# Attention, eight experts and a mixing layer in one kernel: two experts' rows turned by VectorE, and steps re-ordered on three engines

## The chip, the cores and the metric

The program runs on one core of a Trainium2 chip. That core has five engines that run side by side and in order, each through its own queue of instructions: TensorE (PE in the profile; its weight loads are shown apart as PEld), VectorE (DVE), ScalarE (ACT), GpSimd (POOL) and SyncE (SP), which here only starts transfers. Sixteen DMA engines move data between the chip's large memory and the on-chip memory. The metric is the device time of one execution in microseconds; the time of a kernel is the median over its runs.

## The reference

Three stages follow one another: attention, a layer of eight experts in which each token goes to one of them, and a layer that mixes tokens.

```python
# attention: B=2, H=8, S=768, D=64
keep  = is_global | is_local                       # 8 global keys, 96 local ones
a     = softmax(where(keep, q @ k.T * scale - slope * dist, -1e9))
x     = (a @ v) as (B, S, 512)
# experts: E=8, hidden size 1024
logits = x @ w_gate;  local_gate = sigmoid(x @ w_local)
e[s]   = argmax(logits[s]) if s == 0 or local_gate[s] < 0.5 else e[s-1]
x[s]   = softmax(logits[s])[e] * (relu(x[s] @ w1[e]) @ w2[e])
# mixing
theta = x @ w_theta
y     = w_tok_r @ (x cos theta) + w_tok_i @ (x sin theta)
u     = x + y
out   = u + relu(u @ w_ch)
```

The tables of the last stage (w_theta, w_tok, w_ch) arrive as 64-bit floats; the kernel turns them into pairs of 32-bit ones.

## The kernel before

**Attention (0 to about 97 us).** Twelve blocks of 128 tokens. Beside it runs the routing, by pairs of blocks: a chain of small steps that goes back and forth between TensorE and VectorE, two letters each in the list TAIL: `ch` choice, `ro` rows, `sc` scan, `oh` one-hot, `ho`, `po` positions, `pl` place, `mk` marks, `sl` slots, `tk` tokens; `rk` ranks the experts by their number of tokens, `en` writes the lists of tokens (`xidx`) from which rows are gathered.

**The leader (about 96 to 113 us).** When half of the tokens are routed, 128 rows of the expert that then leads are computed ahead. Its hidden layer is cut into eight groups f of 128 units: `ha` and `hb` are the two halves of a first product (L783), `hr` the relu on ScalarE (L788), `ya` and `yb` the two halves of the second product (L794). TAIL writes out by hand in which order these and the last routing steps are issued, and so the order on every engine. Each TensorE product in it waits in TensorE's queue for what it needs, and everything behind it waits too. When `en` has written the lists, GpSimd gathers the first expert's rows (`xg`, L1046), TensorE turns them (`tr`, L1341) and the first expert starts.

**Experts, in order of their number of tokens (115 to 288 us).** Expert r gets at most RCAP[r] = 288, 256, 240, 208, 192, 176, 160, 144 tokens, in tiles of up to 128 rows. Its hidden layer is cut into eight half groups; u = 8r + f counts them from 0 to 63. For each u:

- `mm1` (L1524 for r < 4, L1505 above): the product with w1 into `h`. For r < 4 weights and rows are split into a high and a low part: `w1s` from the loaded `raw` (high part by ScalarE, L1369, low part by VectorE, L1370), and three products.
- `relu`: `hh` by ScalarE (L1553, L1559) and the low part `hl` by VectorE (L1555, L1562); rows beyond the full tile go as `hx` (L1554, L1561).
- `mm2` (L1580): the product with w2, split as `w2s` (`h2`, L1486, by ScalarE; `l2`, L1487, by VectorE), into `o`. For each tile of rows three products follow one another: hh·h2, hh·l2, hl·h2. `mm2_few` (L1596) is the product of the few rows `hx` with `raw`.

For r < 4 the loop goes through u one by one, above it by pairs. TensorE gets the products of u+2 (or u+2 and u+3) ahead of `mm2` of u.

**Rows of the next expert.** `x_tr` at f = 2 and 3 (r < 4) or f = 2 (r of 4 and more) turns a gathered tile of 128 rows x 512 features into features x rows: four products with the identity per tile (L1341) into PSUM and a copy (L1344, L1347, L1349). It then lets GpSimd gather the tile three further on (L1046); three tiles `xg` are held.

**Conversion steps.** `job` is a generator that turns one piece of a 64-bit table into `jw` and then into the split tables (`wth`, `wtokr`, `wch`): per piece two ScalarE steps (L418, L428) and five VectorE steps (L419 to L431). `tick()`, called six times per u (twelve per pair), runs JRATE[r]/4.5 (r of 1 to 3, not at f = 2, 3) or JRATE[r]/6 of a step, so JRATE sets how many of them fall into which expert. A ScalarE step of a job (L428) waits in ScalarE's queue for the VectorE step before it.

**Mixing (290 to 465 us).** For each of twelve blocks the expert results are gathered back from memory (L1774, L1783; for most blocks in four quarters of each row, which VectorE turns in 32 x 32 squares, L1798), and the products of theta (L1843), of the token mixing (L1929) and of w_ch (L1966) follow.

Other names: `yo` is an expert's result on its way to memory (L1631, L1633; stored by GpSimd, L1635), `y` the leader's (L1639), `ps` its tokens' probabilities (L1423), `jraw` the loaded piece of a table.

## Time and profile before

| | before |
|---|---|
| median of 3 runs | 467.28 us (467.28 to 467.78) |
| the profiled execution | 466.93 us, of it span 465.0 us |
| TensorE busy | 457.9 us (98%) |
| VectorE, ScalarE, GpSimd busy | 344.0 (74%), 262.3 (56%), 142.9 us (31%) |

The span runs from the first to the last instruction of the profiled execution. The page's first part gives each engine's busy time, the second cuts the span into 40 slices, the fourth follows the chain that ended last. Times in the rows below are microseconds from the start of the span; "x6" is a number of instructions taken together, and what stands in brackets at a row's end is the idle time before it and what ended that.

### The profile page before, as it was taken

The numbers are of one execution on the slowest core, as the hardware profiler recorded it, in microseconds if no ns is written. First come the engines' busy times: TensorE is split into PE (matmuls) and PEld (weight loads), VectorE is DVE, ScalarE is ACT, GpSimd is POOL, SyncE is SP. The second block draws the span as 40 slices with busy tenths as digits, with TensorE's granted clock in tenths as the row PEclk, the third lists the DMA queues.
The fourth block names the chain that finished last, engine by engine and source line by source line (L and its number), as shares of the span: only waits on it lengthen the run. The fifth ranks groups of instructions, "written<-read, shape, count | busy, mean of one in ns | idle before, by whom it ended". The sixth has DMA issues, their size and how long they took to land.

```text
span 465.0 us, 9578 instructions
## 1 busy us (share of the span) xinstructions
PE 457.9 (98%) x3346; PEld 378.7 (81%) x3346; DVE 344.0 (74%) x946; ACT 262.3 (56%) x623; POOL 142.9 (31%) x203
## 2 busy tenths in 40 slices
PE   8999999999999999999999999999999999999996
PEld 4677777788888898888787788888888888888886
DVE  5888889768687697887888776687997897741522
ACT  5988786822456666655755544556765665630300
POOL 8602313204032404040514302654874441000400
PEclk9999999999999999999999999999999999999999
DMA  8978577715957788788999993521253110000022
GB/s 241 367 231 248 184 240 253 252 47 158 356 167 225 265 296 270 257 277 270 318 348 307 305 312 132 165 91 48 79 152 109 43 49 24 0 35 34 28 87 93
DMA packets 61770, 85.60 MB, mean 184 GB/s; under 512 B 6248, under 2 KB 40296, under 8 KB 61720
## 3 DMA queue, kind: packets, MB, share of 16 engines
q1 hardware_dynamic: 52212, 62.06, 40.8%
q0 software_dynamic: 5552, 12.55, 8.8%
q10 hardware_dynamic: 3956, 10.36, 6.6%
q8 instruction: 27, 0.44, 0.4%
q14 instruction: 23, 0.19, 0.1%
HBM read 73.56 MB, written 11.38 MB: 183 GB/s over the span
## 4 chain that ended last, share of the span: by engine, by line
PE 90%; ACT 4%; DVE 3%; issue 1%; DMA 1%; POOL 0%; DVEq 0%
PE a L1929 22%; PE o L1580 15%; PE h L1524 10%; PE h L1505 8%; PE b L1966 7%; PE th L1843 7%; PE s L574 4%; PE x L653 3%; PE o L1596 3%; PE pt L629 3%; ACT pr L606 2%; PE tr L1341 1%; PE y L670 1%; DVE sm L596 1%; ACT ps L638 1%; PE h L783 1%
## 5 line engine op out<-in xcount | busy, mean ns | idle before, releaser
L1929 PE MATMUL a<-wtokr,z 128*128 128x512 f32 x480 | 85.3, 336 | 0.0
L1929 PEld LDWEIGHTS a<-wtokr,z 128*128 128x128 f32 x480 | 74.2, 188 | 10.0
L1580 PE MATMUL o<-w2s,hh 128*128 128x512 f32 x192 | 62.7, 406 | 0.0
L606 ACT ACTIVATE pr<-sm,st 128x256 f32<-128x256 f32 (+1 forms) x96 | 46.0, 483 | 15.3 <-DVE st L596 15.2
L1524 PE MATMUL h<-xT,w1s 128*128 128x288 f32 (+3 forms) x384 | 51.4, 284 | 0.5 <-DVE xT L1347 0.5
L1524 PEld LDWEIGHTS h<-xT,w1s 128*128 128x128 f32 x384 | 48.7, 189 | 3.4 <-issue 0.6
L1783 POOL DMA_INDIRECT xq<-yd,Lall x40 | 42.4, 1059 | 25.2 <-issue 9.8
L1487 DVE TENSOR_TENSOR w2s<-raw,w2s 128x512 fp32r<-128x512 f32 x56 | 38.5, 689 | 8.4 <-ACT w2s L1486 8.4
L596 DVE CUSTOM_DVE_ANT_0 sm<-s,bias 128x256 f32<-128x256 f32 (+1 forms) x96 | 34.0, 395 | 9.2 <-PE s L574 5.1
L1505 PEld LDWEIGHTS h<-xT,raw 128*128 128x128 f32 x256 | 37.0, 190 | 4.4 <-issue 3.9
L1505 PE MATMUL h<-xT,raw 128*128 128x192 f32 (+3 forms) x256 | 40.5, 311 | 0.0
L1580 PE MATMUL o<-w2s,hl 128*128 128x512 f32 x96 | 38.0, 396 | 0.0
L1580 PEld LDWEIGHTS o<-w2s,hh 128*128 128x128 f32 x192 | 32.4, 184 | 5.8 <-DVE w2s L1487 1.0
L1486 ACT ACTIVATE w2s<-raw 128x512 fp32r<-128x512 f32 x56 | 34.8, 626 | 2.9 <-DMA raw<-in_w_dram 1.4
L1635 POOL DMA_DIRECT2D yd<-yo x13 | 8.2, 634 | 79.1 <-ACT yo L1631 72.4
L1974 DVE SCALAR_TENSOR_TENSOR ob<-b,xTf 128x512 f32<-128x512 f32 (+1 forms) x16 | 8.8, 558 | 29.0 <-PE b L1966 25.7
L1370 DVE TENSOR_TENSOR w1s<-raw,w1s 128x512 fp32r<-128x512 f32 x32 | 22.0, 689 | 6.9 <-ACT w1s L1369 6.4
L574 PE MATMUL s<-kall,q 64*128 64x256 f32 (+1 forms) x192 | 26.1, 391 | 0.0
L629 PE MATMUL pt<-ident,pr 128*128 128x128 f32 x176 | 24.6, 278 | 0.2
L653 PE MATMUL x<-ps,vv 128*64 128x128 f32 x352 | 24.5, 279 | 0.0
L428 ACT ACTIVATE wtokr<-jw 128x512 fp32r<-128x512 f32 x15 | 9.5, 633 | 24.6 <-DVE jw L425 24.6
L1843 PE MATMUL th<-wth,xh 128*128 128x512 f32 x88 | 22.4, 396 | 0.0
(294 smaller groups left out, 944.3 us busy)
## 6 DMA issues: line engine op xcount, KB each, us to landing
raw<-in_w_dram SPq DMA_DIRECT2D x60, 512.0 KB, 5.4
vv<-in_pack_dram SPq DMA_DIRECT2D x10, 512.0 KB, 6.5
jraw<-in_w_tokT_dram ACTq DMA_DIRECT2D x10, 512.0 KB, 5.0
w<-in_w_dram SPq DMA_DIRECT2D x16, 256.0 KB, 5.4
kall<-in_pack_dram SPq DMA_DIRECT2D x10, 320.0 KB, 5.3
xd<-xt SPq DMA_DIRECT2D x12, 256.0 KB, 2.3
q<-in_pack_dram SPq DMA_DIRECT2D x11, 256.0 KB, 4.4
jraw<-in_w_tokT_dram ACTq DMA_DIRECT2D x10, 256.0 KB, 4.7
```

The lines of the kernel that those rows point to most:

```text
L574: PE.matmul(sp[hh][:, 0:W], lhsT=qs[n][half, j], rhs=kall[half, b, j, t * 160 + 160 - W : t * 160 + 160], start=True, stop=True,)
L596: V.tensor_tensor_reduce(out=sm[:, hh, 0:W], in0=ust[u]["s"][hh], in1=bias[:, 2 * j + hh], scale=-0.125, scalar=BIG, op0=ALU.add, op1=ALU.min,
L606: A.activation(pr[:, hh, 0:W], sm[:, hh, 0:W], AF.Exp, bias=st[:, hh : hh + 1], scale=-1.0, accum_out=sums[n][:, 2 * j + hh : 2 * j + hh + 1],
L629: PE.transpose(pt[:, hh, c], pr[:, hh, c * 128 : (c + 1) * 128], ident)
L653: PE.matmul(xp[64 * hh : 64 * hh + 64, j], lhsT=vv[:, i, h * 64 : (h + 1) * 64], rhs=ps[:, hh, c], start=(c == 0), stop=(c == nch - 1),)
L1487: V.tensor_tensor(l2, bb[:, o], f32(h2), op=ALU.subtract)
L1505: PE.matmul(hp[:, :N], lhsT=pieces[u // 2][1][:, j, o * 128 : (o + 1) * 128], rhs=x[:, j, :N], start=(j == 0), stop=(j == 3),)
L1524: PE.matmul(hp[:, :N], lhsT=wa[:, j], rhs=xa[:, j, :N], start=(k == 0), stop=(k == 11))
L1580: PE.matmul(out[:M], lhsT=ha[:, lo : lo + M], rhs=wa, start=(f == 0 and q == 0), stop=(f == 7 and q == 2),)
L1783: G.indirect_dma_start(xq[:, i * 128 : (i + 1) * 128], None, yd.rearrange("n (q w) -> (n q) w", q=4), bass.IndirectOffsetOnAxis(ap=yq[:, i ...
L1843: PE.matmul(th, lhsT=xa[:, j], rhs=wa[:, j], start=(n == 0), stop=(n == 11))
L1929: PE.matmul(acc[b][d][o], lhsT=za[:, d * 128 : (d + 1) * 128], rhs=wa[:, lo:hi], start=(t == 0 and n == 0 and (o == 0 or d % 2 == 0)), sto ...
```

## The change

Five edits stand together.

1. The rows of the last two experts (r of VX = 6 and more) are no longer turned by TensorE. A tile of 128 rows is gathered in four transfers of 128 quarter rows each (a tile of 32 or 16 rows in one), so that the quarters q of 32 rows lie on partitions 32q to 32q+31; one VectorE transpose of 32 x 32 squares per tile writes the rows into `xT`, and there is no copy out of PSUM. Features then lie in another order on the partitions, and w1 of these experts is loaded with rows in the same order. The indices of the quarters are worked out by `quarters`, four VectorE instructions at each u of 2 to 5.
2. JRATE: 1.2 and 1.3 become 1.5 and 1.6 for experts 1 and 2, and 2.7 and 2.3 become 2.3 and 2.1 for experts 4 and 5. The sum of steps stays.
3. In TAIL the leader's half products are cut apart and placed between the routing's products.
4. `mm2` puts hh·h2 of all tiles first and the low products behind them, and takes the two half groups of a pair together.
5. For u of 29 to 31 `split_w2` stands ahead of the ticks; in pairs the six ticks are spread 2, 2, 2 instead of 3, 3, 0.

```diff
-ri11 mk4 ha0 hb0 hr0 jt yt11 lg11 lc11 jt ha1 hb1 hr1 lt11 ld11 ya0 yb0 sl4 ch5 tk4 ha2 hb2 hr2 ro5 sc5 ys11 ya1 yb1 oh5
-ho5 ha3 hb3 hr3 po5 pl5 ya2 yb2 mk5 rk ha4 hb4 hr4 sl5 tk5 ya3 yb3 ha5 hb5 hr5 en ya4 yb4 ha6 hb6 hr6 ya5 yb5 ha7 hb7
+ri11 mk4 ha0 hb0 hr0 jt yt11 lg11 lc11 jt ha1 lt11 ld11 hb1 hr1 ya0 sl4 ch5 tk4 yb0 ro5 sc5 ys11 ha2 hb2 hr2 oh5 ho5
+ya1 yb1 po5 pl5 ha3 hb3 hr3 ya2 mk5 rk sl5 tk5 yb2 ha4 hb4 hr4 ya3 yb3 ha5 hb5 hr5 en ya4 yb4 ha6 hb6 hr6 ya5 yb5 ha7 hb7
...
-JRATE = (2.0, 1.2, 1.3, 3.0, 2.7, 2.3, 0.8)
+JRATE = (2.0, 1.5, 1.6, 3.0, 2.3, 2.1, 0.8)
...
+            order = "o (a p) f -> p (o a) f" if r < VX else "o (p a) f -> p (o a) f"
+            SP.dma_start(p[1], w1[bass.ds(ev, 1), :, c * 256 : (c + 1) * 256].rearrange(order, p=128))
...
+        if r < VX:
+            G.indirect_dma_start(xg[:M], None, xd[:], bass.IndirectOffsetOnAxis(ap=xidx[:M, r, i : i + 1], axis=0))
+            return
+
+        for k in range(-(-M // 32)):
+            idx = xq[:, k, r - VX, i : i + 1] if k < 2 else xq2[:, k - 2, r - VX : r - VX + 1]
+            G.indirect_dma_start(
+                xg[:, k * 128 : (k + 1) * 128],
+                None,
+                xd.rearrange("n (q w) -> (n q) w", q=4),
+                bass.IndirectOffsetOnAxis(ap=idx, axis=0),
+            )
...
+    def quarters(q):
+
+        o = slice(32 * q, 32 * q + 32)
+        for k in range(4):
+            p = slice(32 * k, 32 * k + 32)
+            dst, src = (xq[o, k, 0 : E - VX], xidx[p, VX:E, 0:2]) if k < 2 else (xq2[o, k - 2, 0 : E - VX], xidx[p, VX:E, 0])
+            V.tensor_scalar(dst, src, 4.0, float(q), op0=ALU.mult, op1=ALU.add)
...
+        if r >= VX:
+            k = -(-M // 32)
+            V.transpose(
+                f32(xh[:, :, i * 128 : i * 128 + 32 * k]).rearrange("p j (k a) -> p k j a", a=32),
+                xg[:, 0 : 128 * k].rearrange("p (k c j) -> p k j c", c=32, j=4),
+            )
+            gather_x(n + 3)
+            return
...
-            for i in range(RTILES[r]):
-                lo = i * 128
-                M = min(128, RCAP[r] - lo)
-                if width(r, i) == 128:
-                    out = yps[r][i]
-                    for q, (ha, wa) in enumerate(((hh, h2), (hh, l2), (hl, h2))):
...
+                        prods[0].append((out, hh[:, c], h2, u % 8 == 0, False))
+                        low = [(out, hh[:, c], l2, False, False), (out, hl[:, c], h2, False, u % 8 == 7)]
+                        for k in range(2):
+                            prods[1 if len(us) > 1 else 1 + k].append(low[k])
+            for out, ha, wa, first_, last_ in prods[0] + prods[1] + prods[2]:
+                PE.matmul(out, lhsT=ha, rhs=wa, start=first_, stop=last_)
...
+                    ahead = u + 3 >= 8 * FEW0
+                    if ahead:
+                        split_w2(u + 1)
...
-                mm2(u)
-                mm2(u + 1)
+                mm2(u, u + 1)
...
+            if u in range(2, 6):
+                quarters(u - 2)
```

On TensorE, in the third half group pair of expert 5 (`h` the first product, `tr` the turning of expert 6's two tiles, `o` the second product), before:

```order
L1505 MATMUL h<-xT_3652,raw_3717 128x176 x8
L1341 MATMUL tr<-ident,xg 128x128 x4
L1341 MATMUL tr<-ident,xg 128x32 x4
L1580 MATMUL o<-w2s_3841,hh 128x512
L1580 MATMUL o<-w2s_3842,hh 128x512
L1580 MATMUL o<-w2s_3841,hl 128x512
L1580 MATMUL o<-w2s_3854,hh 128x512
L1580 MATMUL o<-w2s_3855,hh 128x512
L1580 MATMUL o<-w2s_3854,hl 128x512
L1596 MATMUL o<-raw_3729,hx 64x256 x4
```

and now:

```order
L1537 MATMUL h<-xT_3680,raw_3748 128x176 x8
L1618 MATMUL o<-w2s_3865,hh 128x512
L1618 MATMUL o<-w2s_3879,hh 128x512
L1618 MATMUL o<-w2s_3866,hh 128x512
L1618 MATMUL o<-w2s_3865,hl 128x512
L1618 MATMUL o<-w2s_3880,hh 128x512
L1618 MATMUL o<-w2s_3879,hl 128x512
L1628 MATMUL o<-raw_3760,hx 64x256 x4
```

The eight `tr` products are gone (the same at expert 6 for expert 7's tiles), and the two products with a high part on both sides stand first.

On TensorE, in the leader's stretch between the slots of routing step 4 and the positions of step 5 (`small` are routing's products, `h` and `y` the leader's), before:

```order
L783 MATMUL h_1951<-lead_r,w_1416 128x128 x4
L283 LDWEIGHTS rcb
L283 MATMUL small<-identb,rcb 2x128
L284 LDWEIGHTS rcb
L284 MATMUL small<-identb,rcb 2x128
L794 MATMUL y_1931<-w_1416,lead_r 128x256 x2
L302 MATMUL small<-own_80,erow 128x16
L783 MATMUL h_1975<-lead_r,w_1416 128x128 x4
L318 LDWEIGHTS ones
```

and now:

```order
L800 MATMUL y_1931<-w_1416,lead_r 128x256
L286 LDWEIGHTS rcb
L286 MATMUL small<-identb,rcb 2x128
L287 LDWEIGHTS rcb
L287 MATMUL small<-identb,rcb 2x128
L789 MATMUL h_1960<-lead_r,w_1416 128x128 x4
L305 MATMUL small<-own_80,erow 128x16
L800 MATMUL y_1931<-w_1416,lead_r 128x256 x2
L321 LDWEIGHTS ones
```

Each routing product has come forward past half a group or a whole group of the leader's products, which now stand behind it.

On GpSimd, from the gather of expert 5's second tile to the store of the leader's rows, before:

```order
L1046 DMA xg<-xd,xall 48x512
L1046 DMA xg<-xd,xall 128x512
L1635 DMA yd<-yo 128x512
L1635 DMA yd<-yo 80x512
L1417 DMA ps<-pd,toks 128x1
L1423 DMA ps<-pd,toks 128x1
L1046 DMA xg<-xd,xall 32x512
L1046 DMA xg<-xd,xall 128x512
L1423 DMA ps<-pd,sidx 128x1
L1639 DMA yd<-y_107 128x512
```

and now:

```order
L1053 DMA xg<-xd,xall 48x512
L1058 DMA xg<-xd,toks 128x128 x4
L1667 DMA yd<-yo 128x512
L1667 DMA yd<-yo 80x512
L1449 DMA ps<-pd,toks 128x1
L1455 DMA ps<-pd,toks 128x1
L1058 DMA xg<-xd,toks 128x128 x5
L1455 DMA ps<-pd,sidx 128x1
L1671 DMA yd<-y_107 128x512
```

Two gathers of 128 rows have become four each; a store of results, probabilities and the leader's store are queued behind them as before.

## Rows read from the trace of the kernel before

**Rows 1.** The page, part 1: busy time, share of the span, instructions.
```profile
PE 457.9 (98%) x3346; PEld 378.7 (81%) x3346; DVE 344.0 (74%) x946; ACT 262.3 (56%) x623; POOL 142.9 (31%) x203
```
**Rows 2.** The page, part 4: the chain that ended last, by engine.
```profile
PE 90%; ACT 4%; DVE 3%; issue 1%; DMA 1%; POOL 0%; DVEq 0%
```
**Rows 3.** Windows, experts 1, 2, 5, 6: length; busy PE, PEld, DVE, ACT, POOL; clock; DMA share, GB/s.
```profile
140.50:164.60 24.10, 24.10 (x172) 21.42 (x169) 17.98 (x34) 16.36 (x35) 7.71 (x9) 1.00 0.76 248
164.60:187.30 22.70, 22.70 (x154) 20.23 (x153) 19.21 (x37) 14.95 (x32) 5.74 (x6) 1.00 0.84 280
...
232.50:253.40 20.90, 20.90 (x130) 16.43 (x128) 17.13 (x36) 12.86 (x27) 6.65 (x12) 1.00 0.98 330
253.40:272.20 18.80, 18.80 (x155) 15.32 (x153) 14.93 (x38) 9.94 (x20) 4.60 (x7) 1.00 0.91 299
```
**Rows 4.** Timeline of PE, experts 5 and 6: starts of half group pairs.
```profile
237.47 2.65 PE L1505 MATMUL h<-xT,raw 128*128 128x176 f32 x16
...
242.46 2.65 PE L1505 MATMUL h<-xT,raw 128*128 128x176 f32 x16
...
248.44 2.65 PE L1505 MATMUL h<-xT,raw 128*128 128x176 f32 x16
...
262.54 2.44 PE L1505 MATMUL h<-xT,raw 128*128 128x160 f32 x16
...
267.85 2.44 PE L1505 MATMUL h<-xT,raw 128*128 128x160 f32 x16
...
272.18 2.23 PE L1505 MATMUL h<-xT,raw 128*128 128x144 f32 x16
```
**Rows 5.** Groups by line: GpSimd's quarter gathers, a transpose, a small VectorE step.
```profile
L1783 POOL DMA_INDIRECT xq<-yd,Lall x40 | 42.4, 1059 | 25.2 <-issue 9.8 <-DVE xTf L1798 8.5 <-DMA yd<-y 5.7
...
L1798 DVE STREAM_TRANSPOSE xTf<-xq 128x512 f32<-128x512 f32 x10 | 7.1, 706 | 0.3 <-DMA xq<-yd,Lall 0.3
...
L1406 DVE TENSOR_SCALAR Lall<-yidx 32x10 int32<-32x10 int32 x16 | 2.6, 163 | 0.2
```
**Rows 6.** Timeline of DVE, where experts 6's and 7's rows are turned.
```profile
246.93 0.69 DVE L1487 TENSOR_TENSOR w2s<-raw,w2s 128x512 fp32r<-128x512 f32 x1 [0.74 <-ACT w2s L1486]
...
266.72 0.69 DVE L1487 TENSOR_TENSOR w2s<-raw,w2s 128x512 fp32r<-128x512 f32 x1 [2.59 <-ACT w2s L1486]
```
**Rows 7.** Timeline of POOL, experts 4 and 5.
```profile
224.80 1.13 POOL L1635 DMA_DIRECT2D yd<-yo  x2 [17.38 <-ACT yo L1631]
...
230.44 1.11 POOL L1046 DMA_INDIRECT xg<-xd,xall  x1 [0.30 <-PE o L1580]
...
235.13 0.59 POOL L1639 DMA_DIRECT2D yd<-y  x1 [2.33 <-DVE jw L419]
235.71 0.15 POOL L1550 MEMSET hx<- 128x32 f32 x1
```
**Rows 8.** Timeline of PE, first half groups of expert 0.
```profile
119.06 0.79 PE L1580 MATMUL o<-w2s,hh 128*128 128x512 f32 x2
...
120.62 0.89 PE L1580 MATMUL o<-w2s,hh 128*128 128x512 f32 x2
...
121.58 0.64 PE L1580 MATMUL o<-w2s,hh 128*128 128x512 f32 x2
```
**Rows 9.** Timeline of PEld, end of expert 3 and start of 4.
```profile
201.54 1.42 PEld L1524 LDWEIGHTS h<-xT,w1s 128*128 128x128 f32 x12 [0.25 <-ACT w1s L1369]
...
218.91 0.19 PEld L1580 LDWEIGHTS o<-w2s,hl 128*128 128x128 f32 x1 [0.27 <-DVE hl L1555]
```
**Rows 10.** Timeline, all engines, from the leader to the first expert.
```profile
108.80 1.03 POOL L1046 DMA_INDIRECT xg<-xd,xall  x1 [4.89 <-DVE om L845]
113.26 0.60 PE L1341 MATMUL tr<-ident,xg 128*128 128x128 f32 x4
114.08 0.99 PE L1341 MATMUL tr<-ident,xg 128*128 128x128 f32 x8 [0.22 <-DMA xg<-xd,xall]
115.54 3.69 PE L1524 MATMUL h<-xT,w1s 128*128 128x288 f32 x24 [0.47 <-DVE xT L1347]
```

More of the change, by code (lines that the diff above doesn't have):

```diff
@@ L52 @@
 VT = 2
+VX = 6
 NRAW = 3
@@ L455 @@
     prow = toks.rearrange("p i w e -> p (i w e)")[:, 0:25].bitcast(I32)
+    xq = toks.rearrange("p i w e -> p (i w e)")[:, 25:41].bitcast(I32).rearrange("p (k r i) -> p k r i", k=2, i=2)
+    xq2 = toks.rearrange("p i w e -> p (i w e)")[:, 41:49].bitcast(I32).rearrange("p (k r) -> p k r", k=2)
     y0 = ct([128, DM], F32, "y0")
@@ L1029, in load_piece @@
             p[1] = pre.tile([128, 4, 256], F32, tag="raw1", name="raw1", bufs=NRAW)
-            SP.dma_start(
-                p[1], w1[bass.ds(ev, 1), :, c * 256 : (c + 1) * 256].rearrange("o (a p) f -> p (o a) f", p=128)
-            )
+            order = "o (a p) f -> p (o a) f" if r < VX else "o (p a) f -> p (o a) f"
+            SP.dma_start(p[1], w1[bass.ds(ev, 1), :, c * 256 : (c + 1) * 256].rearrange(order, p=128))
         if 2 in parts:
@@ L1045, in gather_x @@
         M = min(128, RCAP[r] - i * 128)
-        G.indirect_dma_start(xg[:M], None, xd[:], bass.IndirectOffsetOnAxis(ap=xidx[:M, r, i : i + 1], axis=0))
         xgs[n] = xg
+        if r < VX:
[9 more added lines that the diff above has]
+            )
     pieces[0] = {2: pre.tile([128, 2, DM], F32, tag="raw2", name="raw2", bufs=NRAW)}
@@ L1333, in x_tr @@
         xg = xgs.pop(n)
+        M = min(128, RCAP[r] - i * 128)
+        if r >= VX:
[6 more added lines that the diff above has]
+            return
         if r > 1 and i:
@@ L1338, in x_tr @@
             tp = (pR_[0] if r else pZ).tile([128, 4, 128], F32, tag="tr", name="tr")
-        M = min(128, RCAP[r] - i * 128)
         for j in range(4):
@@ L1565, with mm2 @@
         yps, fews = {}, {}
-        def mm2(u):
-            r, f = divmod(u, 8)
+        def mm2(*us):
+            r, f = divmod(us[0], 8)
             if f == 0:
                 yps[r] = [pO.tile([128, DM], F32, tag="o", name="o") for _ in range(RTILES[r] - (r == E - 1))]
-            h2, l2, w = wsp2.pop(u)
-            hh, hl, hx = hts.pop(u)
-            fews[u] = hx, w
-            for i in range(RTILES[r]):
-                lo = i * 128
-                M = min(128, RCAP[r] - lo)
-                if width(r, i) == 128:
-                    out = yps[r][i]
-                    for q, (ha, wa) in enumerate(((hh, h2), (hh, l2), (hl, h2))):
-                        PE.matmul(
-                            out[:M],
-                            lhsT=ha[:, lo : lo + M],
-                            rhs=wa,
-                            start=(f == 0 and q == 0),
-                            stop=(f == 7 and q == 2),
-                        )
+            prods = [[], [], []]
+            for u in us:
+                h2, l2, w = wsp2.pop(u)
+                hh, hl, hx = hts.pop(u)
+                fews[u] = hx, w
+                for i in range(RTILES[r]):
+                    if width(r, i) == 128:
+                        c = slice(i * 128, min(i * 128 + 128, RCAP[r]))
+                        out = yps[r][i][: c.stop - c.start]
+                        prods[0].append((out, hh[:, c], h2, u % 8 == 0, False))
[4 more added lines that the diff above has]
+                PE.matmul(out, lhsT=ha, rhs=wa, start=first_, stop=last_)
         def mm2_few(u, out=None):
@@ L1693 @@
                 else:
+                    ahead = u + 3 >= 8 * FEW0
+                    if ahead:
+                        split_w2(u + 1)
+                    if u == 8 * FEW0 - 1:
+                        split_w2(u + 2)
                     tick()
@@ L1697 @@
                     tick()
-                    split_w2(u + 1)
-                    if u == 8 * FEW0 - 1:
-                        split_w2(u + 2)
+                    if not ahead:
+                        split_w2(u + 1)
                     tick()
@@ L1722 @@
                 split_w2(u + 2)
-                for _ in range(3):
+                for _ in range(2):
                     tick()
                 relu(u + 3)
-                for _ in range(3):
+                for _ in range(2):
                     tick()
                 split_w2(u + 3)
+                for _ in range(2):
+                    tick()
                 if u == SU:
```

## The prediction, made before the changed kernel ran

> **What bounds the kernel now.** I read the busy times first: TensorE is busy for 457.9 of 465.0 us [rows 1]. The chain of work that ended last says the same from the other side: 90% of it is TensorE's own instructions, one after the other, and only 4% and 3% are ScalarE's and VectorE's [rows 2]. Then I cut the experts' stage into windows. In experts 1, 2, 5 and 6 TensorE's busy time is equal to the length of the window, to the second decimal, at a granted clock of 1.00, the upper of its two levels [rows 3]. So in that stage a TensorE product that goes away is worth its whole duration, and a step moved on another engine is worth nothing as long as no TensorE product waits for it. The question for each edit is therefore only: does TensorE get less work, and does something that it needs come later than TensorE reaches it?
>
> The timelines show the few places where TensorE does wait: at the start of the first expert (0.22 and 0.47 us, [rows 10]), in the first second products of expert 0, which take longer than their like [rows 8], and a few loads of weights around the passage from expert 3 to 4 [rows 9].
>
> **Turning of the last two experts' rows.** In the timeline of expert 5 a pair of half groups without turning takes 242.46 - 237.47 = 4.99 us, the next one, which turns expert 6's two tiles, 248.44 - 242.46 = 5.98. In expert 6 the pair that turns expert 7's tiles takes 267.85 - 262.54 = 5.31, the next one without 272.18 - 267.85 = 4.33 [rows 4]. The differences, 0.99 and 0.98, are what the eight products with the identity cost each time. They go, and nothing takes their place on TensorE: **-1.97 us**.
>
> What the edit puts elsewhere:
> - VectorE gets two transposes per expert. One of 128x512 takes 706 ns [rows 5]; the smaller tile has a quarter of it or less. That is some 0.9 us per expert, where VectorE stands idle for 0.74 us ahead of one step in expert 5 and 2.59 in expert 6 [rows 6], and where it is busy 17.13 of 20.90 and 14.93 of 18.80 [rows 3]. The new transpose reads with a stride, which no row shows: I take 0.71, bounds 0.7 and four times that, 2.8. Even 2.8 us once per expert would mostly be absorbed; what is not is in the last term below.
> - GpSimd's gather of a tile of 128 rows becomes four. A quarter gather takes 1059 ns [rows 5], and between two 0.30 us pass [rows 7]. The first four fall at the start of the 17.38 us in which GpSimd stands idle before 224.80. The second four replace the gather at 230.44: they end near 230.44 + 4 x 1.36 = 235.9 instead of 231.6, and behind them are queued a gather of probabilities, the leader's store (at 235.13 before) and the clearing of `hx` (235.71) [rows 7]. With 1.3 us for the probabilities the store starts at about 237.2 and the clearing ends at about 238.1, 2.3 us later than before. TensorE needs this `hx` at the end of the pair that ends at 242.46 [rows 4], so some 3 us are left: nothing.
> - `quarters` adds 16 small VectorE instructions in expert 0, of 163 ns by the nearest row [rows 5], 2.6 us over four half groups. No row of mine shows VectorE's idle time there; I cost it at nothing, and up to 0.4 in the last term.
>
> **Conversion steps (JRATE).** Experts 1 and 2 run 48 - 12 = 36 ticks that count, so 0.3 more means 0.3 x 36 / 4.5 = 2.4 steps more each; expert 4 has 0.4 x 48 / 6 = 3.2 fewer, expert 5 1.6 fewer. The total is the same. A step works on 128x512 numbers, as the ones of 0.69 us do [rows 6]: at most 2.4 x 0.69 = 1.7 us more for VectorE in experts 1 and 2, which then is busy 19.7 of 24.10 and 20.9 of 22.70 us [rows 3]. It still fits, though in expert 2 only 1.8 us of idle time are left. On the other side the DMA engines, which are busy 0.98 and 0.91 of the time in experts 5 and 6 against 0.76 and 0.84 in experts 1 and 2 [rows 3], get some of the loads of tables earlier. Nothing by itself, since TensorE doesn't wait in any of these windows.
>
> **Order of the second products.** The low part `l2` now is needed one or two products later. In expert 0's first half groups two products took 0.79 and 0.89 us where two unhindered ones take 0.64 [rows 8]: 0.15 + 0.25 = 0.40 is what `l2` cost. Most of it goes, but the second wait is of the same kind, so what is late next is the same `l2` by a rest: **-0.25**, bounds -0.40 and 0.
>
> **`split_w2` ahead and ticks spread.** It aims at the waits of 0.25 and 0.27 us at the passage from expert 3 to 4 [rows 9]. They stand in the row of the weight loads, so TensorE lost no more than these. Putting `split_w2` ahead makes the conversion steps and `split_w1` later by one step of 0.69 on VectorE. **-0.2**, bounds -0.5 (both waits gone) and +0.4 (one new wait in place of it, of half a step).
>
> **TAIL.** Routing's products come forward past a half group or a group of the leader. The nearest row for such a half group is four products of 128x128, 0.60 us [rows 10], so the lists of tokens come about one such piece, 0.6 to 0.9, earlier, and with them the first gather at 108.80. But the first expert can't start before the leader's products are through: TensorE's work between is the same, and it ends at 113.26 where the first turning starts. Only what is lost after it can be saved: 0.22 at 114.08 and, in part, 0.47 at 115.54 [rows 10]; the second of these is the wait for VectorE's copy of what has just been turned and stays. Against it, a routing product that has come forward may stand there before its operand is ready, and then the leader's products behind it wait too. Bounds: -0.69 (both waits gone) and +0.6 (one half group's time lost). I take **-0.15**, near the smaller wait.
>
> **New waits** from VectorE's added work, by the bounds above: between 0 and 1.0 us, of which I take **+0.1**, since every window still has idle time on VectorE.
>
> **Sum.** -1.97 - 0.25 - 0.2 - 0.15 + 0.1 = -2.47. The profiled execution took 466.93 us, span 465.0 and 1.93 around it; so 464.46. The median of the runs is 467.28, 0.35 above the profiled one: **464.8 us**.
>
> **Rivals.**
> - *Given back to the transfers.* In expert 5 the DMA engines are busy 0.98 of the window [rows 3]. If weights arrive there just in time, the pair that is 0.99 shorter ends in a wait for `raw`, and perhaps the same in expert 6: 464.8 + 0.99 to 464.8 + 1.97, say 466.3. For it: that share. Against it: TensorE waits nowhere in the window, and loads of tables move out of it.
> - *The leader's stretch gives all.* If both waits of [rows 10] go: 464.8 - 0.54 = 464.3. Against it: the second one is a copy that must follow the turning.
> - *Gathers slowed by VectorE.* GpSimd's gathers could take longer beside a busy VectorE. With twice the time of each, the four end at 230.44 + 4 x 2.42 = 240.1, the clearing of `hx` at 242.3, about when TensorE asks for it; with three times it is 4.2 us later. Between the two the price is some 2.5 us: 467.3. Against it: the forty gathers that now run beside VectorE have a mean of 1.06 us, and the one at 230.44 took 1.11 [rows 5, 7]. The Trainium skill ("SBUF — State Buffer", section "SBUF: two separate sides") warns of just this: descriptors of a DMA issued by GpSimd can't be written while VectorE runs an instruction that takes both of its ports, and it gives about 620 ns for such a DMA alone and 3100 beside a VectorE copy; by that factor of five as an estimate the last of four gathers would come some 17 us later and the time be above 475. By the row with mean 1.06 the trace does not bear that factor out.
> - *VectorE falls behind: slower.* The mechanism: VectorE's idle time in experts 1 and 2, 6.1 and 3.5 us [rows 3], is not spare but the waits of the splits for ScalarE and for TensorE's results. Then each added step pushes the next `l2`, `w1s` or `hl` back, and TensorE waits for it. It decides once the lag is more than the idle time that really is free. If none is: 1.7 x 2 + 2.6 = 6.0, less the 1.1 us (1.6 steps) that expert 5 gets back, 4.9: 464.8 + 4.9 = 469.7. Against it: TensorE meets no wait at all in the two windows now, so there is some lead.
>
> **How the numbers follow.** My forecast, with its own range of 464.0 to 465.8, gets 0.62; the transfers 0.18, of which two thirds end below 466.35; the leader 0.10; the gathers 0.05; VectorE behind 0.05. About 0.2% (0.93 us) is what a measurement of this kernel can tell from no change, so faster means below 466.35 and slower above 468.21. Faster: 0.62 + 0.10 + 0.11 = 0.83; same: 0.07 and 0.04 of the gathers, 0.11; slower 0.05 + 0.01 = 0.06. With all terms at their good ends the sum is -1.97 - 0.40 - 0.5 - 0.69 = -3.6, so 463.7; with the transfers' rival included up to 466.5 no more than 2 in 10 are left out.
>
> **What would show it.** Right: in expert 5 and 6 all pairs of a length near 4.99 and 4.33 and no `tr`; the new transposes near 0.7 us; the first second products of expert 0 at 0.64 for two; expert 1's and 2's windows still with TensorE busy all through; the first expert's first product at 115.2 to 115.6 instead of 115.54. Wrong: waits of TensorE for `l2`, `w1s` or `hl` in experts 0 to 2; waits for `raw` in experts 5 and 6; a clearing of `hx` later than 241; a transpose of 2 us or more. If the time comes out at 466.5 or above, the turning was not worth its 1.97 or another wait has taken it back.

## The result: slower, and the profile after

The changed kernel takes 470.04 us (median of 7 runs, 469.12 to 471.2), the kernel before 467.28 (466.63 to 468.3): ratio 1.0057, 95% interval 1.0039 to 1.0075. That is 2.76 us more, where 2.5 us less were forecast, and outside the range of 463.7 to 466.5.

The page of the kernel after, parts 1 and 4 (to be held against [rows 1, 2]):

```profile
PE 457.6 (98%) x3330; PEld 377.6 (81%) x3330; DVE 349.3 (75%) x966; ACT 260.8 (56%) x619; POOL 149.0 (32%) x209
...
PE 74%; DVE 7%; DMA 7%; ACT 6%; issue 4%; POOL 1%; ACTq 0%; SPq 0%; DVEq 0%; POOLq 0%
```

TensorE has sixteen products fewer and is busy as long as before. The share that says something is the other one: of the chain that ended last, TensorE had 90% and now has 74%. Most of the rest is VectorE, transfers and ScalarE. So the kernel got new waits, and the windows by expert (experts 1 to 6; columns as in [rows 3]) tell where:

```profile
140.45:165.09 24.64, 24.45 (x172) 21.54 (x169) 19.60 (x41) 15.73 (x33) 7.86 (x9) 1.00 0.74 246
165.09:188.06 22.97, 22.96 (x153) 20.14 (x152) 19.91 (x38) 15.56 (x33) 5.25 (x6) 1.00 0.86 281
188.06:212.19 24.13, 23.39 (x154) 19.54 (x153) 20.68 (x39) 15.10 (x33) 7.90 (x8) 1.00 0.85 276
212.19:235.59 23.40, 22.15 (x127) 17.61 (x125) 17.67 (x36) 14.23 (x28) 7.03 (x9) 1.00 0.77 257
235.59:255.56 19.97, 19.97 (x123) 15.69 (x121) 16.56 (x33) 10.16 (x20) 10.05 (x15) 1.00 0.99 322
255.56:273.35 17.79, 17.79 (x146) 14.50 (x144) 16.55 (x42) 9.89 (x21) 5.27 (x7) 1.00 1.00 328
```

Experts 5 and 6 are 0.93 and 1.01 us shorter, as forecast. Experts 3 and 4, where nothing was forecast but 0.2 us of gain, are longer than TensorE's busy time by 0.74 and 1.25 us. In expert 2 busy time and window still agree (22.96 of 22.97), and yet 0.26 us is lost there (from half group 17 to 18, below): a product that waits for its weights can count as busy.

A finer instrument for this is TensorE's lag: the start of the first product of each half group, after minus before. It is flat wherever TensorE does the same work without new waits, and a step in it is a wait or work gained or lost, with its place. For the kernel after it reads: +0.23 at half group 0, -0.03 at 13 (the new order of the second products), +0.39 at 14, +0.71 at 18, +0.81 at 28, **+1.78 at 29**, **+3.13 at 36**, +2.13 at 46 and +1.17 at 54 (the two turnings that went), **+1.79 at 60**, +1.94 at 62, +2.43 at the first product of the token mixing, 2.48 in the products of w_ch and 2.63 at the end of the span.

The forecast rows first. TensorE's pairs without turning (experts 5 and 6, against [rows 4]):

```profile
240.59 2.65 PE L1537 MATMUL h<-xT,raw 128*128 128x176 f32 x16
245.57 2.65 PE L1537 MATMUL h<-xT,raw 128*128 128x176 f32 x16
250.57 2.66 PE L1537 MATMUL h<-xT,raw 128*128 128x176 f32 x16
...
264.67 2.44 PE L1537 MATMUL h<-xT,raw 128*128 128x160 f32 x16
269.01 2.44 PE L1537 MATMUL h<-xT,raw 128*128 128x160 f32 x16
273.35 2.23 PE L1537 MATMUL h<-xT,raw 128*128 128x144 f32 x16
```

Every pair now takes 4.98 to 5.00 and 4.34 us: the lag falls by 0.98 and 0.96 where the turnings were. What took over the work, by groups of lines (VectorE's transposes, GpSimd's quarter gathers, `quarters`; against [rows 5]) and GpSimd's timeline (against [rows 7]):

```profile
L1058 POOL DMA_INDIRECT xg<-xd,toks x10 | 11.2, 1121 | 3.0 <-issue 1.5 <-PE h L1556 0.3 <-DVE w2s L1519 0.3
...
L1347 DVE TENSOR_SCALAR toks<-xall 32x4 int32<-32x4 int32 (+1 forms) x16 | 3.0, 188 | 0.3
L1361 DVE STREAM_TRANSPOSE xT<-xg 128x512 f32<-128x512 f32 (+1 forms) x4 | 2.9, 754 | 0.1
```

```profile
240.34 0.59 POOL L1671 DMA_DIRECT2D yd<-y  x1
240.91 0.21 POOL L1582 MEMSET hx<- 128x32 f32 x2
```

A gather beside VectorE takes 1.12 us instead of 1.06, so nothing of a factor of two. The large transposes took 1.15 us, not the 0.71 of [rows 5], but within the bounds. The clearing of `hx` ends at 241.1, and TensorE asks for it at the end of the pair that ends at 245.57. Both parts held.

Now the two large steps. At half group 29, ScalarE's and TensorE's timeline:

```profile
201.54 0.63 ACT L431 ACTIVATE wtokr<-jw 128x512 fp32r<-128x512 f32 x1 [2.47 <-DVE jw L428]
...
202.08 0.67 ACT L1663 ACTIVATE yo<-o,ps 112x512 f32<-112x512 f32 x1
...
202.65 0.62 ACT L1401 ACTIVATE w1s<-raw 128x512 fp32r<-128x512 f32 x1
...
203.32 1.37 PE L1556 MATMUL h<-xT,w1s 128*128 128x208 f32 x10 [0.73 <-ACT w1s L1401]
```

ScalarE stood for 2.47 us at a conversion step whose VectorE part had not come. The next result (`yo`) and the split `w1s` stood behind it, and TensorE waited for that split. In the kernel before ScalarE stands almost as long, but earlier, and the split starts 2.42 us after that step and not 1.11:

```profile
198.45 0.64 ACT L428 ACTIVATE wtokr<-jw 128x512 fp32r<-128x512 f32 x1 [2.19 <-DVE jw L425]
...
200.87 0.62 ACT L1369 ACTIVATE w1s<-raw 128x512 fp32r<-128x512 f32 x1
```

At half group 36, all engines:

```profile
216.94 0.63 ACT L431 ACTIVATE wtokr<-jw 128x512 fp32r<-128x512 f32 x1 [2.81 <-DVE jw L428]
...
218.60 1.29 DVE L1519 TENSOR_TENSOR w2s<-raw,w2s 128x512 fp32r<-128x512 f32 x2 [1.69 <-ACT w2s L1518]
...
219.81 0.69 DVE L434 TENSOR_TENSOR wtokr<-jw,wtokr 128x512 fp32r<-128x512 f32 x1
...
220.53 0.43 DVE L422 TENSOR_SCALAR jw<-jraw 128x512 int32<-128x512 int32 x1
...
220.99 0.69 DVE L424 SCALAR_TENSOR_TENSOR jw<-jraw,jw 128x512 int32<-128x512 int32 x1
...
221.80 0.41 DVE L1587 SCALAR_TENSOR_TENSOR hl<-h,hh 128x256 fp32r<-128x256 f32 x1
...
222.27 0.50 PE L1618 MATMUL o<-w2s,hl 128*128 128x512 f32 x1 [1.25 <-DVE hl L1587]
```

VectorE first waits 1.69 us for ScalarE's high part of `w2s`, then does three conversion steps, and only then the `hl` that TensorE is waiting for. In the kernel before the same place reads:

```profile
215.36 0.43 DVE L419 TENSOR_SCALAR jw<-jraw 128x512 int32<-128x512 int32 x1
...
215.82 0.69 DVE L421 SCALAR_TENSOR_TENSOR jw<-jraw,jw 128x512 int32<-128x512 int32 x1
...
216.43 1.28 DVE L1487 TENSOR_TENSOR w2s<-raw,w2s 128x512 fp32r<-128x512 f32 x2
217.64 0.68 DVE L423 SCALAR_TENSOR_TENSOR jw<-jraw,jw 128x512 int32<-128x512 int32 x1
...
218.44 0.42 DVE L1555 SCALAR_TENSOR_TENSOR hl<-h,hh 128x256 fp32r<-128x256 f32 x1
```

There two conversion steps fill the time that VectorE now spends waiting, and one stands in front of `hl`. (TensorE then waited 0.27 us by [rows 9].)

Of the smaller steps, those seen at half groups 14 and 18:

```profile
157.94 0.37 ACT L1665 ACTIVATE yo<-o,ps 128x128 f32<-128x128 f32 x1 [3.38 <-DMA yd<-yo]
...
168.10 1.31 PEld L1556 LDWEIGHTS h<-xT,w1s 128*128 128x128 f32 x11 [0.31 <-DVE w1s L1402]
```

At 14 ScalarE waits for the store of an earlier result to land, and the split `w1s` that TensorE needs stands behind. Every run has this wait of ScalarE; the experiments tell how its length varies. Ahead of 18 a weight load waits for the low part of `w1s`; only the five runs with the new rates have this loss (0.26 to 0.33).

### The profile page after: what moved, and what is told of

The parts are those of the page before. It is cut to its first block, busy times and chain, and to the rows that moved or that the text cites. A ratio compares the mean times of both kernels' runs of the same rounds, so it can differ in the third digit from the quotient of the medians.

```text
span 467.7 us, 9567 instructions
## 1 busy us (share of the span) xinstructions
PE 457.6 (98%) x3330; PEld 377.6 (81%) x3330; DVE 349.3 (75%) x966; ACT 260.8 (56%) x619; POOL 149.0 (32%) x209
## 4 chain that ended last, share of the span: by engine, by line
PE 74%; DVE 7%; DMA 7%; ACT 6%; issue 4%; POOL 1%; ACTq 0%; SPq 0%; DVEq 0%; POOLq 0%
PE a L1969 21%; PE o L1618 8%; PE b L2006 7%; PE th L1883 7%; PE h L1556 7%; PE h L1537 5%; PE s L580 3%; PE x L659 3%; DMA yd<-yo 3%; PE pt L635 3%; ACT pr L612 2%; DMA late<-in_w_dram 2%; PE o L1628 2%; PE y L676 1%; PE y L800 1%
## 5 line engine op out<-in xcount | busy, mean ns | idle before, releaser
L1618 PE MATMUL o<-w2s,hh 128*128 128x512 f32 x192 | 58.0, 409 | 0.1
L1618 PE MATMUL o<-w2s,hl 128*128 128x512 f32 x96 | 32.9, 396 | 1.3 <-DVE hl L1587 1.3
L1618 PEld LDWEIGHTS o<-w2s,hl 128*128 128x128 f32 x96 | 17.6, 184 | 6.5 <-DVE hl L1587 2.1
```

The source lines that it names most:

```text
L1618: PE.matmul(out, lhsT=ha, rhs=wa, start=first_, stop=last_)
```

## The experiments

**Theory A**: the moved conversion steps and the splits put ahead of the ticks make the losses up to half group 36. **Theory B**: the order of splits and ticks alone does. **Theory L** (formed after e8): what the turning gives is lost again in expert 7, because the last weights `late` (expert 7's w2) land no earlier. The lag in us at some half groups, and at the first product of the token mixing, is in this table (each one profiled execution, against one of the kernel before):

| run | 13 | 28 | 29 | 36 | 45 | 53 | 57 | 63 | mixing | ratio of times, 95% |
|---|---|---|---|---|---|---|---|---|---|---|
| after | -0.03 | 0.81 | 1.78 | 3.13 | 3.11 | 2.13 | 1.17 | 1.94 | 2.43 | 1.0057 (1.0039 to 1.0075) |
| e1 old rates | -0.22 | 0.07 | 0.05 | 1.04 | 1.25 | 1.36 | 0.39 | 0.98 | | 1.0015 (1.0002 to 1.0028) |
| e2 old splits, ticks | -0.10 | 1.02 | 2.61 | 3.77 | 3.75 | 2.77 | 1.80 | 2.08 | | 1.0033 (1.0017 to 1.0050) |
| e3 old second products | -0.01 | 1.01 | 2.51 | 4.10 | 4.07 | 3.10 | 2.14 | 2.50 | | 1.0055 (1.0040 to 1.0070) |
| e4 turning alone | -0.13 | 0.37 | 0.37 | 0.55 | 0.52 | 0.17 | -0.79 | -0.71 | | 1.0001 (0.9979 to 1.0022) |
| e5 before again | -0.37 | -0.37 | -0.37 | -0.37 | -0.40 | -0.38 | -0.38 | -0.38 | -0.21 | 0.9999 (0.9985 to 1.0012) |
| e6 old rates, old ahead | -0.30 | 0.10 | 0.08 | 0.00 | -0.02 | -0.77 | -1.73 | -0.74 | 0.11 | 0.9993 (0.9978 to 1.0008) |
| e7 old rates, splits, ticks | -0.15 | -0.13 | -0.15 | -0.21 | -0.23 | -0.55 | -1.50 | -0.69 | 0.14 | 0.9998 (0.9989 to 1.0007) |
| e8 shift of a whole piece | -0.25 | 0.62 | 0.94 | 2.15 | 2.14 | 1.16 | 0.19 | 0.82 | 1.76 | 1.0036 (1.0021 to 1.0051) |
| e9 as e6, late early | -0.12 | -0.11 | -0.13 | -0.17 | -0.20 | -1.17 | -2.13 | -1.56 | -0.68 | 0.9976 (0.9964 to 0.9988) |
| e10 before, late early | 0.18 | 0.28 | 0.28 | 0.27 | 0.25 | 0.25 | 0.25 | 0.25 | 0.42 | 0.9992 (0.9983 to 1.0001) |
| e11 after, late early | -0.25 | 0.41 | 1.36 | 2.69 | 2.69 | 1.71 | 0.74 | 1.15 | 2.21 | 1.0040 (1.0027 to 1.0053) |
| e12 ahead alone | -0.38 | -0.38 | -0.38 | 0.77 | 0.74 | 0.75 | 0.75 | 0.74 | 0.80 | 1.0021 (1.0010 to 1.0032) |
| e13 turning alone, again | -0.43 | -0.43 | -0.42 | 0.13 | 0.11 | -0.20 | -1.17 | -0.45 | | 1.0005 (0.9992 to 1.0019) |
| e14 second products alone | -0.33 | 0.07 | 0.04 | -0.14 | -0.17 | -0.17 | -0.17 | 0.02 | | 1.0006 (0.9993 to 1.0018) |

e1 to e4 ran on one chip, e13 and e14 on another, and on both every kernel, that before too, has a median of 478.7 to 481.5 us: TensorE loses some 12 us more from 293 us on (last section). Their ratios are against the kernel before on the same chip, and their lags are read up to half group 63, ahead of that place.

**e1, old rates.**

```diff
-JRATE = (2.0, 1.5, 1.6, 3.0, 2.3, 2.1, 0.8)
+JRATE = (2.0, 1.2, 1.3, 3.0, 2.7, 2.3, 0.8)
```

> The changed kernel with the old table of rates of the conversion steps (1.2 and 1.3 for experts 1 and 2, 2.7 and 2.3 for 4 and 5), all else as changed. In the trace of the changed kernel TensorE falls back against the kernel before by 0.42, 0.25 and 0.08 us in experts 1 and 2, by 0.97 at half group 29 and by 1.42 at half group 36. Theory A (the moved conversion steps come to stand ahead of splits and low parts, and ScalarE's queue waits behind a conversion step): the first four losses go, 1.7 us, and most of the 1.42 too, so 467.0 to 468.3 us. Theory B (the new order of the splits and ticks does it): only the 0.75 of experts 1 and 2 goes, the losses at 29 and 36 stay, 469.3 us.

The lag grows by 0.29 up to half group 28 instead of 0.84, and by nothing at 29 instead of 0.97; at 36 there are 0.99 left of 1.35. So A holds for the losses up to 29 and fails for most of the one at 36. New losses turn up in experts 5 and 6: from 36 to 53 the lag grows by 0.32 although the first turning gives 0.98 there, so 1.30 are lost, the largest of them waits of weight loads for `l2` (0.56, 0.38 and 0.66). There VectorE has its old conversion steps in pairs that are now shorter. Of the runs with the turning, those with the new rates lose nothing at 46 to 50, and those with the old ones 0.2 to 1.1, but for e9, which loses nothing.

**e2, old splits and ticks.** At half groups 29 to 31 `split_w2` again behind the second tick, in pairs three ticks, three ticks, none.

> The changed kernel with the old places of the w2 splits at half groups 29 to 31 and the old 3, 3, 0 ticks in pairs. Theory A (moved conversion steps): the losses up to half group 29 stay to the hundredth, that at 36 stays within 0.3 us, 470.0 us. Theory B (order of splits and ticks): the 1.42 at half group 36 goes, 468.6 us.

With the new rates the loss from 29 to 36 falls from 1.35 to 1.16, while that at 29 grows from 0.97 to 1.59. Neither theory as written: B's whole 1.42 does not go, and A's losses up to 29 do not stay to the hundredth. With the new rates, then, the old order gives nothing back.

**e3, old second products.** `mm2(u)` and `mm2(u + 1)`, three products per tile.

> The changed kernel with the old order of the second products (three per tile, one half group after the other). Theory A: 470.0 to 470.3 us, with 0.25 us lost in expert 0 and nothing given back later. Rival: in pairs the new order asks for the second half group's high part two products earlier and so makes the waits at half group 36 and in expert 7; then 1 to 2 us less, 468 to 469.

The gain of 0.24 at half group 2 goes, and nothing comes back at 36 (1.59). Expert 7 costs 0.36 instead of 0.77, but TensorE comes there 0.97 later and ends it later, at 2.50. Theory A; the rival falls.

**e4, turning alone.** The kernel before with edit 1.

> The kernel before with nothing but the two last experts' rows turned by VectorE. Theory A (the products that went are a gain of 1.94 us, and the later losses of 1.30 us in expert 7 come from the last weights that land no earlier): -1.94 + 0.9 to 1.3, 466.0 to 466.3 us. Rival (the losses in expert 7 come from the late start of expert 6 and 7 and the new order): the whole -1.94 stays, 465.3 us.

By half group 57 the 1.94 us are there, less 0.48 lost at 14, 0.16 at 34 and 0.63 in experts 5 and 6. Expert 7 then costs only 0.08 (e13 has 0.72 with the same kernel). The ratio's interval is too wide to tell the two expectations apart, and what follows 293 us can't be read on this chip.

**e5, the kernel before again.**

> All five edits undone in the changed kernel's text: instruction for instruction the kernel before, for a trace of it on the same chip as the runs beside it. Every theory: no difference in time beyond noise (ratio 0.999 to 1.001); a loss of 0.3 to 0.5 us of TensorE around half group 14 that it shares with the run in which only the rows are turned by VectorE would show that loss to belong to the chip and not to the turning.

No difference in time, and no loss at 14. That loss comes and goes between executions of one kernel: e4 has 0.48 and e13 none. It goes by the store: ScalarE's wait for it, shown above, is 2.64 to 3.01 us in the seven traces with a loss of at most 0.05 and 3.17 to 3.54 in the nine with 0.21 or more. All five runs with the new rates are among the nine, and four of the eleven with the old ones, so a share of the rates isn't excluded. What this trace also gives is the size of chance: -0.34 at the start of the first expert, for the same instructions.

**e6, old rates and old places of the splits at 29 to 31.**

```diff
-                    ahead = u + 3 >= 8 * FEW0
-                    if ahead:
-                        split_w2(u + 1)
...
                     tick()
+                    split_w2(u + 1)
```

> The changed kernel with the old rates and the old places of the w2 splits at half groups 29 to 31; ticks in pairs stay 2, 2, 2, the new order of the second products, the turning and TAIL stay. With the old rates alone TensorE still lost 1.04 us at half group 36, waiting for a low part hl behind two w2 low parts and three conversion steps on VectorE. Theory A1 (splits ahead of the ticks leave VectorE idle while it waits for ScalarE's w2s, and push the conversion steps that would have filled that time in front of hl): that loss falls to under 0.2 us, time 0.8 to 1.0 us below the run with old rates alone. Theory A2 (the new order of the second products or the spread ticks make it): it stays at 0.8 to 1.1.

At 36 the loss of 0.99 is gone, to -0.08: A1 holds. TensorE is 1.73 us ahead at half group 57, and at the mixing 0.11 behind.

**e7, old rates, splits and ticks.**

> The changed kernel with old rates, old splits and old ticks in pairs: only the turning, the new order of the second products and TAIL stay. Theory A: no loss over 0.3 us at half groups 28 to 36; what is left of the gain of 1.94 us is lost in experts 5 and 6, where VectorE now has the old conversion steps in shorter pairs (0.5 to 1.4 us, waits for l2 at half groups 42 to 50); time 0.5 to 1.2 us below the kernel before. Rival: the new order of the second products alone costs in pairs, then more is lost than in the run with only the turning (0.63 us there), and the time is no better than before.

As theory A had it up to half group 57 (-1.50, with 0.66 lost at 46 to 50); but the time is that of before, since 0.81 is lost in expert 7 and 0.83 before the mixing. The rival's figure came out, by another mechanism. In the chain of e6 the loss in expert 7 can be followed:

```profile
265.00 10.15 DMA late<-in_w_dram
...
275.26 0.64 ACT w2s L1518
...
276.54 0.68 DVE jw L424
277.22 0.10 DVE y L1586
277.32 0.33 DVE hl L1587
277.65 0.61 DVE w2s L1519
...
278.30 0.73 PE o L1618 x2
```

The load of the last expert's w2 takes 10.15 us from its issue at 265.00, and with a conversion step and `hl` in VectorE's queue between the two low parts it ends in a wait of TensorE. The first split of it starts at 275.34 in e5, 275.26 in e6, 275.32 in e7 and 275.30 in e4; TensorE's first product with it starts at 277.90, 276.55, 276.77 and 277.49. TensorE comes earlier, the weights don't. ScalarE's queue holds expert 6's last result `yo` behind these splits (276.66, 276.58, 276.64, 276.62).

All traces together say it more sharply. In ten (after, e1 to e4, e6 to e8, e13, e14) the first product of half group 63 starts 8.08 to 8.10 us after the first split of `late`, whatever the lag: there the landing, and what follows from it, sets the pace. In the kernel before, e5 and e12 it starts 9.08, 8.37 and 9.18 after it, so TensorE could come earlier only by 1.0, 0.3 and 1.1 us before it met that bound; with `late` issued earlier (e9 to e11) it is 11.7 to 11.9. From issue to first split it takes 9.3 to 10.6 us in these thirteen, so how much of a turning is lost also varies from execution to execution (e4, e13).

**e8, a shift of a whole piece.** `JRATE = (2.0, 1.6375, 1.7375, 3.0, 2.2625, 1.8625, 0.8)`.

> The changed kernel with 1.6375 and 1.7375 for experts 1 and 2 and 2.2625 and 1.8625 for experts 4 and 5: 3.5 steps more in each of experts 1 and 2 than before, 7 in all, which is one whole piece, so that expert 3 meets the same steps in the same places as in the kernel before. Theory P (the loss of 0.97 us at half group 29 comes from which step falls there): that loss goes, under 0.3 us, while experts 1 and 2 lose more than the 0.8 us of the changed kernel. Theory Q (it comes from VectorE being behind after more work in experts 1 and 2): 0.97 or more stays.

More steps in experts 1 and 2 than in the changed kernel, and the loss at 29 is 0.32, not 0.97. Theory P rather than Q, though just above P's bound: most of what costs is which step falls in front of which split. Experts 1 and 2 lose hardly more than in the changed kernel (0.87 against 0.84), which P did not have. The loss at 36 stays (1.21).

**e9, as e6, with late one pair earlier.**

```diff
-                load_piece(u // 2 + NRAW, (2,))
+                n = u // 2 + NRAW
+                if n < NPC - 4:
+                    load_piece(n, (2,))
+                if NPC - 5 <= n:
+                    load_piece(n + 1, (2,))
```

> The changed kernel with old rates and old split places (the run before with both of these took the same time as the kernel before), and the four loads of the last expert's w2 (late) each issued one pair of half groups earlier. Theory L (the gain of the turning is lost because late lands at about 275.3 us however early TensorE gets there, and ScalarE's queue holds the last store of expert 6 behind it): late lands 2 to 5 us earlier, the losses of 0.84 and 0.15 us in expert 7 and of 0.85 before the mixing go for the greater part, 465.0 to 465.7 us, ratio 0.996 to 0.997. Rival M (the transfers are full there, late takes as much longer as it is issued earlier, or the raw weights ahead of it come later): no more than 0.3 us better than before, ratio 0.999 to 1.0005.

466.04 against 467.01 us, the best of all: ratio 0.9976, between what L and M gave. The first split of `late` starts at 270.68 and TensorE keeps 1.56 us to half group 63: the losses at 60 and 62 are gone, as L had it. But M has a share: 0.61 is lost at 58 in a wait for raw weights, which are now issued behind `late`, and 0.88 before the mixing. From half group 57 to the mixing 1.45 is lost, against 1.84 in e6 and 1.64 in e7; so the earlier issue itself is worth 0.2 to 0.4. The rest of its lead over e6 was there at 57 (-2.13 against -1.73), 0.32 of it the store at 14. The intervals of e9 and e6 overlap. The chain of e9:

```profile
263.84 10.81 DMA raw<-in_w_dram
...
274.79 2.20 PE h L1537 x16
...
287.59 2.02 DMA yd<-yo
...
290.38 4.32 DMA yg<-yd,yidx
...
294.84 1.08 PE b L1847 x32
```

**e10, the kernel before with late early** (the same edit).

> The kernel before with only the loads of late one pair earlier. Theory L: TensorE waits for nothing there before the change, so no gain over 0.3 us, ratio 0.999 to 1.0005; it is the control for the run beside it. Rival (late was a brake already before the change): 0.5 to 1 us less.

No gain that can be told: the lag stays flat from 28 to 63. As a control it says that the load is no brake in the kernel before.

**e11, the changed kernel with late early.**

> The changed kernel, all five edits, with late one pair earlier. Theory L: the losses of 0.62, 0.15 and 0.49 us from half group 60 to the mixing go, those at half groups 14 to 36 stay; 468.7 to 469.3 us, ratio 1.003 to 1.0045. Rival M: 469.8 or more.

1.0040, within what L gave. In expert 7 the 0.77 become 0.41; before the mixing 1.06 is lost instead of 0.49, which L had not.

**e12, splits ahead alone.**

> The kernel before with one thing of the change: at half groups 29 to 31 the w2 splits stand ahead of the ticks. Theory A1 (it pushes conversion steps between the w2 low parts and the low part hl): TensorE loses 0.7 to 1.4 us at half group 36, ratio 1.001 to 1.003 (part of it is taken up by waits in expert 7). Rival: without the new order of the second products and the spread ticks it costs nothing, and the 1.04 us were of the three together.

1.15 us lost at 36 and nowhere else by half group 63, ratio 1.0021. A1: this part by itself makes the kernel slower, though VectorE's idle time is another one than in the changed kernel:

```profile
215.38 0.69 DVE L434 TENSOR_TENSOR wtokr<-jw,wtokr 128x512 fp32r<-128x512 f32 x1 [0.70 <-ACT wtokr L431]
...
219.68 0.50 PE L1613 MATMUL o<-w2s,hl 128*128 128x512 f32 x1 [1.06 <-DVE hl L1585]
```

A conversion step of VectorE, put behind a split, makes ScalarE's step late and VectorE wait 0.70 us for it; then two conversion steps stand between the splits and `hl`, where the kernel before has one. e1 shows the same (0.70, two steps), e6 neither.

**e13, turning alone, and e14, the second products alone.**

> The kernel before with only the last two experts' rows turned by VectorE, once more, to see it through the mixing. Theory L (late and the last results set the end of the experts): TensorE is 1.4 to 1.9 us ahead at half group 58, loses 0.3 to 0.9 in expert 7 and 0.5 to 0.9 before the mixing; 466.6 to 467.1 us, ratio 0.998 to 1.0005. Rival (the losses in expert 7 belong to the new order of the second products): nothing lost there, 465.6 to 466, ratio 0.996 to 0.9975. For the gather of results: 4.3 us if it goes with the turning, 3.7 if not.

> The kernel before with only the new order of the second products. Forecast term: 0.24 us gained in expert 0, as in every run with it. If the order costs nothing in pairs, TensorE keeps it to the mixing: ratio 0.9985 to 1.0. If in pairs it makes waits in expert 7 (the second half group's high part is asked for two products earlier): 0.2 to 0.8 us lost at half group 60 and 62, ratio 1.0 to 1.0015. The gather of results lands in 3.7 us if its 4.3 goes with the turning, in 4.3 if with this order.

In e13 TensorE is 1.17 ahead at 57, less than L's 1.4 to 1.9, and loses 0.72 in expert 7, with the old order of the second products: L, and the rival falls; 0.55 at 34 and 0.66 at 48 to 50 are lost besides. In e14 the 0.23 at half group 2 is there; 0.32 is lost at 14 and 0.19 in expert 7, and the time is that of before. It has no turning, but its `late` lands latest after its issue (10.6 us) and is the bound here too. The landing of the gather can't be read in either, so that question stays open.

## Why the prediction was wrong, step by step

- **Turning: the size right, its worth wrong.** Forecast -1.97, measured -0.98 and -0.96. What failed is the sentence that a product that goes away is worth its whole duration, because TensorE is busy all through these windows. That is true of the window and not of what follows it: the issue of `late` waits for products ahead of the second turning (in e5 it comes at 265.21, the turning runs from 264.44 to 265.39), so the 0.96 falls between what releases the issue and the use, and only makes TensorE come early. In the rival "given back to the transfers" I looked for `raw` in expert 5; the transfer was `late` in expert 7. Of the 1.94 us 1.26 were lost again there and before the mixing (+0.62, +0.15, +0.49), and in e7, where experts 1 to 4 lose nothing, 1.64. What the share before the mixing comes from is open (below).
- **Conversion steps: "nothing by itself" failed.** They cost 1.5 us up to half group 29 (after against e1: 1.81 and 0.27 from half group 13 on), or 1.3 without the loss at 14 (0.42 and 0.21), which the length of a store decides. On the other side the new rates avoid the loss that the old ones have beside the turning at half groups 46 to 50 (0.2 to 1.1, in e9 nothing). I compared VectorE's busy time with the window; what counted is the place of each step in two queues. ScalarE's step waits for VectorE's, and the splits behind it wait too. The term that should have held this, new waits at +0.1 with a bound of 1.0, was too small. The rival "VectorE falls behind: slower" has part of that mechanism; I gave it 0.05 and placed it in experts 1 and 2, which account for 0.84, with the 0.42 at 14. That its 469.7 lies near the measured 470.04 is luck: it is added up from other losses. The larger part came in expert 3, whose rate was not changed: the shift of 4.8 steps put other steps in front of its splits (e8).
- **Splits ahead: the sign failed.** Forecast -0.2, measured +1.15 alone (e12) and +1.07 in e1 against e6 (0.99 and -0.08 from 29 to 36). I priced it as a reordering of a busy queue. But VectorE's steps wait for ScalarE's and ScalarE's for VectorE's, and a wait moved forward leaves VectorE idle, with conversion steps that had filled that time now in front of `hl` (1.69 us idle and three steps in the changed kernel, 0.70 and two in e12 and e1). The effects don't add up: beside the new rates the old order is no better (e2: 2.75 lost at 29 to 36, against 2.32).
- **Second products: right.** Forecast -0.25, measured -0.23 to -0.25 at half group 2 in each run that has them, 0.00 to -0.02 in each that has not. Rows of the changed kernel, against [rows 8]; a row is now two products hh·h2 and two hh·l2, and only the second still holds a wait (1.28, where the first takes 1.09):

```profile
119.29 1.09 PE L1618 MATMUL o<-w2s,hh 128*128 128x512 f32 x4
...
120.68 1.28 PE L1618 MATMUL o<-w2s,hh 128*128 128x512 f32 x4
```

- **TAIL: no gain seen.** Forecast -0.15 at the first expert's start. Nine profiles with the new TAIL start it at -0.03 to +0.23 (mean +0.08), seven with the old at -0.43 to +0.20 (mean -0.17). The spread of equal instructions (-0.34 in e5) is as large, so that it costs 0.2 is likely and not shown. What failed is clear, though: that TensorE's work before the first turning ends where it did. In the nine the first gather starts at 107.91 to 108.17 instead of 108.66 to 108.96, so the lists do come earlier, as forecast; but the first turning starts at 113.64 to 113.89 instead of 113.12 to 113.42. And the wait for `xg` that the edit was to save stands in only two of the seven old ones. The changed kernel's rows, against [rows 10]: the wait for `xg` of 0.22 is gone, but the leader's products end 0.6 us later.

```profile
113.89 1.40 PE L1373 MATMUL tr<-ident,xg 128*128 128x128 f32 x12
115.77 3.69 PE L1556 MATMUL h<-xT,w1s 128*128 128x288 f32 x24 [0.47 <-DVE xT L1379]
```

- **GpSimd and `quarters` at nothing: right.** The clearing of `hx` ended at 241.1, which is 238.0 with the kernel's lag of 3.1 taken off, 238.1 by my working; no wait for `quarters` shows in expert 0, where the lag is flat from half group 3 on.

The measured sum, by the lag: +0.23 (start) - 0.26 (second products) + 0.84 (experts 1 and 2) + 0.97 (half group 29) + 1.35 (to 36) - 1.96 (turning) + 0.77 (expert 7) + 0.49 (before the mixing) = 2.43, and 0.2 to the end. (In the chances of the prediction two thirds of 0.18 are 0.12 and not 0.11; nothing hangs on it.)

Still open: before the mixing, 0.8 to 1.1 us are lost in e6 to e9 and e11, of which 0.64 to 0.84 is a wait for the first gather of results, `yg`. It lands 4.27, 4.37 and 4.32 us after its issue in e6, e8 and e9, and 3.65, 3.82 and 3.71 in the kernel before, e10 and e12. Turning, second products or TAIL: not settled.

## What to carry to other kernels

Removed work on a saturated engine is worth what the next fixed arrival leaves of it: look behind the window for a transfer whose issue is released ahead of the saving and which is used after it. Moving its issue forward can help (e9), but it delayed other loads and here gave back only 0.2 to 0.4 of some 1.7 us. In an engine that works in order, a wait put ahead of filler work can cost twice, once as idle time and once as filler in front of what is urgent (e1, e12). Shifting a periodic filler by part of its period changes its phase in the stages that follow, also those whose rate is untouched (e8).

## What the runs showed of the hardware

- TensorE stood still without a wait that the profile shows (`issue`). On the chip of e13, in the run of 64 and 32 small products before the mixing:

```profile
293.15 1.39 PE L1631 MATMUL few<-late,y 128*32 128x128 f32 x41
...
298.44 0.65 PE L1631 MATMUL few<-late,y 128*32 128x128 f32 x4 [1.01 <-issue]
```

  One to four products, then up to 1.5 us of nothing, until 305.6; its granted clock has fallen to 0.50 (1.2 GHz) from 300 to 310, from 1.00 before. In e5 on another chip the same products go at 1.00, the 64 without a gap. The cause is open: a lack of instructions would look like this, but the trace's transfer of the next instructions starts at 292.77 and takes 1.07 us in e13, 292.14 and 1.34 us in e5.
- A VectorE transpose of 128x512 whose source is read with a stride of four elements took 1.15 us (at 249.32 in the kernel after); those of the mixing, with a contiguous source, took 0.71 [rows 5].
- A quarter gather took 6.4 us from issue to landing (4.9 to 7.4, ten of them), in the experts where the DMA engines are busy 0.77 to 1.00.
